# Tail keys of the attention's AV product as half-height matmuls, in a T5-bias attention and FFN kernel

## The chip, the cores and the metric

The kernel runs on one core of one Trainium2 chip. The metric is the device time of one execution in microseconds; the median of several runs is compared. Reported beside it are the span of the profiled execution (first to last instruction) and the clock that TensorE was granted.

## The reference

Eight batches of eight heads, 576 positions and 64 values a head, T5-style bias by distance, then a two-layer FFN with a leaky ReLU. Cut to what is computed:

```python
scores = q @ k.transpose(0, 1, 3, 2) / sqrt(64)          # (8, 8, 576, 576)
scores = scores + bias_table[bucket(abs(i - j))]         # constant beyond a distance of 128
attn = softmax(scores)
x = (attn @ v).transpose(0, 2, 1, 3).reshape(4608, 512)
h = x @ w_in                                             # 512 -> 2048
out = maximum(0.01 * h, h) @ w_out                       # 2048 -> 512, float32
```

## The kernel before

**Tiling of the attention.** Work goes by pairs of heads: `items` lists 32 pairs, `n` from 0 to 31, four to a batch. Scores stand transposed, keys on partitions and queries along the free dimension. The 576 keys are four chunks of 128 (`NJ = 4`) and a tail of 64 (`SL`). Per pair, `score(n, u)` makes six units: units 0 to 3, one for each full chunk, are two matmuls (one for each head) on partitions 0 to 63 and 64 to 127 of `kt` and `qt` (the head dimension is 64); unit 4 is the last 64 queries against the full chunks; unit 5 is the tail keys of both heads, 64 partitions each, against all queries. `expo(n, u)` is the exponential on ScalarE: units 0 to 4 go to the buffer `at`, unit 5 to `at4`, where the lower 64 partitions hold head 0's tail keys and the upper 64 head 1's. The bias is multiplied in afterwards by `band(n, c)` on VectorE. There are two `at`/`at4` buffers, used by turns.

**AV.** `av(n, e)` makes the output of one head `e`: five blocks of 128 queries (`NJ + 1`), each a chain of four matmuls over full key chunks (`L480`) and one over the tail keys (`L482`), 65 columns wide: 64 values and a column of ones that gives the softmax sum. The tail matmul uses all 128 partitions of `at4` and a `v4` whose half for the other head is zero. The chain is closed by the tail (`stop=True`). The output lies in one PSUM bank, `ps_o`, of a pool of one; only in batch 0 does head 1 take a bank `ps_om` of the pool `m` of three. `norm(n, e)` on VectorE takes the reciprocal of the sums (`L491`) and multiplies (`L492`) into `opair`. The result is turned into `xT` by a DMA on SP's queue (`x_dma`) or by TensorE (`x_pe`, `L506`, with a copy `L510`).

**FFN.** Nine tiles `T` of 512 tokens. `ffn_in(T, f)` is four matmuls of 512 columns (`L523`) into a bank of the pool `m`; ScalarE turns it into `gt` (`L528`). `ffn_out(T, ts, i)` is a quarter of the 16 matmuls (`L535`) that make 128 tokens of the output, in another bank of `m`; VectorE copies it out (`L540`) and SP stores it.

**Transposes of q and k.** `rows`, `turn_by_pe` (TensorE, `L395`, through two banks of `m`) or, for pairs 10 and later, `turn_by_dma` (SP), then `take_turned` (`L407`) and `apart` (`L411`).

**Order.** The order of all engines is made by the class `Plan`: every task has an engine, a cost in microseconds, tasks that must precede it, a rank, and PSUM slots that it takes and gives (`S`: the two score slots of two banks each, `O`: the bank `ps_o`, `M`: the banks of pool `m`). `order()` always takes the task that can start first by these numbers, and by rank among equals; so FFN blocks fill the time between a pair's tasks. `plan_pair(n)` adds a pair's scores (from pair 4 on in three tasks of two units), exponentials, bands, the two AVs (cost 0.78 each, after everything of the pair is done) and divisions. `user_before(n)` names the pair whose `at` buffer pair `n` uses again.

Of the kernel before, what the change touches and what calls it, by code (L numbers as in the profile page):

```python
# [10 lines left out]
FP32 = mybir.dt.float32  # L11
# [25 lines left out]
class Plan:  # L37
# [8 lines left out]
    def add(self, engine, cost, after, go, rank, take=(), give=(), tail=0.0, at=None):  # L46
        t = {"engine": engine, "cost": cost, "after": list(after), "go": go, "rank": rank, "n": len(self.tasks),
             "take": list(take), "give": list(give), "tail": tail, "end": at, "start": at}
        if at is None:
            self.tasks.append(t)  # L50
        return t
# [71 lines left out]
def kernel(  # L123
# [10 lines left out]
    nc = tc.nc  # L134

    B, H, S, D = q.shape
# [4 lines left out]
    P = 128  # L141
    n_pairs = H // 2
    NJ = S // P
    SL = S - NJ * P
# [19 lines left out]
    ps_o_pool = ctx.enter_context(tc.tile_pool(name="ps_o", bufs=1, space=bass.MemoryType.PSUM))  # L164
    ps_m_pool = ctx.enter_context(tc.tile_pool(name="ps_m", bufs=3, space=bass.MemoryType.PSUM))
# [11 lines left out]
    NBUF = 2  # L177
# [5 lines left out]
    v4 = [per.tile([P, n_pairs, 2, D + 1], BF16, name=f"v4_{i}") for i in range(NBUF)]  # L183
# [179 lines left out]
    items = [(b, p) for b in range(B) for p in range(n_pairs)]  # L363
    N = len(items)
    NQT = 3
    qts, kts, opairs, prs, turned, scores, outs = {}, {}, {}, {}, {}, {}, {}
# [7 lines left out]
    def x_by_dma(n):  # L374
        return n_pairs + 2 <= n < N - 1 and n != 2 * n_pairs - 1
# [40 lines left out]
    def at_buf(n):  # L416
        if n == 2:
            return spare
        i = n if n < 2 else (n + 1) % 2
        return at_[i], at4_[i]  # L420
# [4 lines left out]
    def score(n, u):  # L425

        qt, kt = qts[n], kts[n]
        ps = scores[n, u] = ps_s_pool.tile([P, 2, 512], FP32, name="ps_s")
        if u < NJ:
            for e in range(2):  # L430
                r = slice(e * D, (e + 1) * D)
                nc.tensor.matmul(ps[:, e, :], lhsT=kt[r, u * P : (u + 1) * P], rhs=qt[r, 0:512],  # L432
                                 start=True, stop=True)
        elif u == NJ:
            for c in range(NJ):
                nc.tensor.matmul(ps[:, 0, c * P : (c + 1) * P], lhsT=kt[:, c * P : (c + 1) * P],  # L436
                                 rhs=qt[:, S : S + P], start=True, stop=True)
        else:
            nc.tensor.matmul(ps[:, 0, :], lhsT=kt[:, S : S + P], rhs=qt[:, 0:512], start=True, stop=True)  # L439
            nc.tensor.matmul(ps[:, 1, 0:SL], lhsT=kt[:, S : S + P], rhs=qt[:, 512:S], start=True, stop=True)  # L440
# [14 lines left out]
    def band(n, c):  # L455
# [8 lines left out]
            m = mirrored(hk[:, 2 * p : 2 * p + 2, :], lo - (c - 1) * P, hi - (c - 1) * P)  # L464
        nc.vector.tensor_tensor(out=o, in0=o, in1=m, op=ALU.mult)  # L465

    def av(n, e):

        b, p = items[n]
        i = b % NBUF  # L470
        at, at4 = at_buf(n)
        if b == 0 and e == 1:
            ps = ps_m_pool.tile([P, NJ + 1, D + 1], FP32, name="ps_om", tag="m")
        else:
            ps = ps_o_pool.tile([P, NJ + 1, D + 1], FP32, name="ps_o", tag="ps_o")
        outs[n, e] = ps
        for ic in range(NJ + 1):
            for c in range(NJ):
                o = (e * NJ + c) * S + ic * P
                nc.tensor.matmul(ps[:, ic, :], lhsT=at[:, o : o + P], rhs=vn[i][:, c, 2 * p + e, :],  # L480
                                 start=(c == 0), stop=False)
            nc.tensor.matmul(ps[:, ic, :], lhsT=at4[:, ic * P : (ic + 1) * P], rhs=v4[i][:, p, e, :],  # L482
                             start=False, stop=True)

    def norm(n, e):

        ps = outs.pop((n, e))
        if e == 0:
            opairs[n] = op_pool.tile([P, NJ + 1, 2 * D], BF16, name="opair")
        rcp = rc_pool.tile([P, NJ + 1, 1], FP32, name="rcp")  # L490
        nc.vector.reciprocal(rcp, ps[:, :, D : D + 1])  # L491
        nc.vector.tensor_tensor(out=opairs[n][:, :, e * D : (e + 1) * D], in0=ps[:, :, 0:D],  # L492
                                in1=rcp.to_broadcast([P, NJ + 1, D]), op=ALU.mult)
# [37 lines left out]
    def ffn_out(T, ts, i):  # L531
        if i == 0:
            ys[T, ts] = ps_m_pool.tile([P, DM], FP32, name="pm2", tag="m")
        for f in range(4 * i, 4 * i + 4):
            nc.tensor.matmul(ys[T, ts], lhsT=gts[T][:, f, ts * P : (ts + 1) * P], rhs=w_out_sb[:, f, :],  # L535
                             start=(f == 0), stop=(f == n_fc - 1))
# [11 lines left out]
    add = plan.add  # L548
    L = {}
    rowt, cut, sct, ext, avt, nmt, xt, vt = {}, {}, {}, {}, {}, {}, {}, {}  # L550
# [72 lines left out]
    def user_before(n):  # L623
        return None if n < 3 else (n - 3 if n < 5 else n - 2)

    order_s = []

    def plan_pair(n):
        b, p = items[n]
        rank = 10 * n  # L630
        soon = rank - (25 if n == n_pairs - 1 else 0)
        cq, ck, aq, ak = cut[n]
        need = {4: [aq, ck], 5: [ak, cq]}
        units = [[u] for u in range(6)] if n < n_pairs else [[0, 1], [2, 3], [4, 5]]
        ac = [0.95, 0.95, 0.95, 0.95, 0.52, 0.56]
        m = user_before(n)
        before = avt[m] if m is not None else []
        es, ss = {}, []
        for us in units:
            ds = [d for u in us for d in need.get(u, [cq, ck])]  # L640
            if n >= PACE and us[0] == 0:
                j = 4 * (n - 4) - LEAD
                if j >= 0:
                    ds.append(("in", j // n_fc, j % n_fc))
            t = add("PE", 0.3 * len(us), ds + before + order_s[-1:],
                    lambda us=us: [score(n, u) for u in us], rank + (-25 if n < n_pairs else 2), take=["S"] * len(us))
            order_s.append(t)
            ss.append(t)
            for u in us:
                es[u] = add("ACT", ac[u], [t], lambda u=u: expo(n, u), rank + 2, give=["S"])  # L650
        sct[n] = ss
        cost = [0.43, 0.56, 0.56, 0.48, 0.25]
        bt = [add("DVE", cost[c], [es[u] for u in ([c], [c], [c], [3, 4], [5])[c]] + [L["hk", 0 if n == 0 else 1]],
                  lambda c=c: band(n, c), soon + 3) for c in range(NJ + 1)]
        done = list(es.values()) + bt + [vt[b]]
        old = xt.get(n - 2, [])
        avs, nms = [], []
        for e in range(2):
            k = "M" if b == 0 and e == 1 else "O"
            avs.append(add("PE", 0.78, done, lambda e=e: av(n, e), soon + 4, take=[k]))  # L660
            nms.append(add("DVE", 0.68, [avs[-1]] + old + nms, lambda e=e: norm(n, e), soon + 3, give=[k]))
        avt[n] = avs
        if x_by_dma(n):
            xt[n] = [add("SP", 0.1, nms, lambda: x_dma(n), soon + 4, tail=6.0)]
            nmt[n] = xt[n]
        else:
            xt[n] = [add("PE", 0.3, nms, lambda: x_pe(n), soon + 4, take=["M"])]
            nmt[n] = [add("DVE", 0.45, xt[n], lambda: x_copy(n), soon + 3, give=["M"])]
# [11 lines left out]
    def plan_ffn(T):  # L680
        last = (T * TT + TT - 1) // S
        need = [t for p in range(n_pairs) for t in nmt[last * n_pairs + p]]
        acts = []
        for f in range(n_fc):
            i = ins[T, f] = add("PE", 0.866, need + [L["w_in", int(f >= n_fc // 2)]] + (oin[T - 2] if T > 1 else []),
                                lambda f=f: ffn_in(T, f), 10000 + T * 64 + f * 4, take=["M"])
            acts.append(add("ACT", 0.54, [i], lambda f=f: ffn_act(T, f), 10000, give=["M"]))
        oin[T] = []
        for ts in range(TT // P):
            last_p = []  # L690
            for i in range(4):
                rank = 10000 + (T + 1) * 64 + (ts * 4 + i) * 4 + 2
                last_p = [add("PE", 0.866, acts + [L["w_out", i // 2]] + last_p, lambda ts=ts, i=i: ffn_out(T, ts, i),
                              rank, take=["M"] if i == 0 else [])]
                oin[T] += last_p
            y = add("DVE", 0.69, last_p + ([yts[-4]] if len(yts) > 3 else []), lambda ts=ts: ffn_y(T, ts), 0, give=["M"])
            yts.append(add("SP", 0.1, [y], lambda ts=ts: ffn_store(T, ts), 10000, tail=2.5))
# [7 lines left out]
    for T in range(n_tt):  # L705
        plan_ffn(T)
# [40 lines left out]
```

## Time and profile before

| | us |
|---|---|
| runs | 393.38, 394.59, 392.37 |
| median of the three | 393.38 |
| profiled execution | 393.96 |
| its span | 392.2 |
| granted TensorE clock over the span | 0.984 |
| full-chunk AV matmuls from the two `at` buffers into `ps_o` (`L480`) | 1180 instructions |
| tail matmuls of the same (`L482`) | 295 instructions |

Times in the profile are microseconds unless marked ns. Engines: PE is TensorE's matmuls, PEld its weight loads (they overlap with PE), DVE is VectorE, ACT is ScalarE, POOL is GpSimd, SP is SyncE, and SPq a DMA queue's issuer. `L480` is line 480 of the kernel before. A line `ps_o<-vn,at 128*128 128x65` names output and inputs, the rows and columns of the array that are used, and the moving operand. Matmuls are pipelined: the length of one is not the distance from one to the next. A `<-` behind an idle time names what ended it.

### The profile page before, as it was taken

The page shows a single profiled execution, that of the slowest core. Times are in us where ns is not written, and L with a number is a line of the kernel's source. Part 1 is how long each engine was busy: PE and PEld are TensorE (multiplying, and loading weights), DVE is VectorE, ACT ScalarE, POOL GpSimd, SP SyncE. Part 2 cuts the span into 40 slices and gives each one's busy share as a digit, 9 for nine tenths or more (in the row PEclk, how much of TensorE's full clock was granted, in tenths as well). Part 3 has the DMA queues.
Part 4 walks back from the last instruction along what each step waited for, and adds up shares of the span by engine and source line. Part 5 has one row for each costly group of instructions (what it writes and reads, how often), then busy time and mean ns, then how long its engine had stood idle before and what let it go on. Part 6 is the DMA issues. An engine that isn't in the chain of part 4 may idle for free.

```text
span 392.2 us, 8305 instructions
## 1 busy us (share of the span) xinstructions
PE 376.5 (96%) x3388; PEld 191.6 (49%) x3388; DVE 202.8 (52%) x539; ACT 243.6 (62%) x345; POOL 68.8 (18%) x112
## 2 busy tenths in 40 slices
PE   7849899999999999999999999999999999999995
PEld 2437355555455454545545555555555444444442
DVE  6637657886776666668567755555433201001021
ACT  3936689548966898688777766666675333333300
POOL 7267404043005201600700220000000000000000
PEclk8978999999999999999999999999999999999998
DMA  7969999779949984997995591111111010101012
GB/s 127 217 112 180 207 207 166 132 104 173 172 98 111 179 117 79 159 158 111 122 157 123 80 133 45 45 43 45 46 43 46 31 51 27 55 27 53 28 53 80
DMA packets 102741, 40.62 MB, mean 104 GB/s; under 512 B 81704, under 2 KB 97072, under 8 KB 102704
## 3 DMA queue, kind: packets, MB, share of 16 engines
q0 software_dynamic: 48512, 17.47, 40.8%
q1 hardware_dynamic: 53984, 22.33, 28.4%
q8 instruction: 26, 0.43, 0.4%
q10 hardware_dynamic: 208, 0.29, 0.3%
q14 instruction: 11, 0.09, 0.1%
HBM read 37.69 MB, written 9.45 MB: 120 GB/s over the span
## 4 chain that ended last, share of the span: by engine, by line
PE 89%; SPq 3%; DVE 2%; DMA 2%; ACT 1%; POOL 1%; issue 0%; DVEq 0%; POOLq 0%
PE pm L535 32%; PE pm L523 32%; PE ps_o L480 10%; PE ps_s L432 8%; PE ps_o L482 2%; SPq L312 2%; PE ps_s L436 2%; PE ps_s L439 2%; DMA tab<-in_bias_table_dram 1%; DMA first<-in_v_dram 1%; ACT at L446 1%; DVE opair L492 1%; POOL vn L333 1%; DVE at L465 1%; PE ps_t L395 0%; PE ps_om L480 0%
## 5 line engine op out<-in xcount | busy, mean ns | idle before, releaser
L523 PE MATMUL pm<-xT,w_in_sb 128*128 128x512 bf16 x576 | 145.0, 379 | 1.5 <-ACT gt L528 1.0
L535 PE MATMUL pm<-w_out_sb,gt 128*128 128x512 bf16 x576 | 143.3, 379 | 0.0
L446 ACT ACTIVATE at<-ps_s 128x1024 bf16<-128x1024 f32 x124 | 120.2, 1023 | 26.8 <-PE ps_s L432 25.6
L528 ACT ACTIVATE gt<-pm 128x512 bf16<-128x512 f32 x144 | 86.1, 601 | 75.4 <-PE pm L523 74.5
L535 PEld LDWEIGHTS <-gt 128*128 128x128 bf16 x576 | 52.7, 98 | 66.0 <-issue 8.9
L523 PEld LDWEIGHTS <-w_in_sb 128*128 128x128 bf16 x576 | 52.5, 98 | 64.2 <-issue 6.9
L465 DVE TENSOR_TENSOR at<-at,hk 128x768 bf16<-128x768 bf16 (+3 forms) x155 | 68.0, 453 | 24.5 <-ACT at L446 14.6
L540 DVE COPY y<-pm 128x512 f32<-128x512 f32 x36 | 24.8, 690 | 82.2 <-PE pm L535 81.7
L480 PEld LDWEIGHTS <-at 128*128 128x128 bf16 x1240 | 53.4, 99 | 22.2 <-issue 8.9
L480 PE MATMUL ps_o<-vn,at 128*128 128x65 bf16 x1180 | 54.7, 195 | 4.5 <-POOL vn L333 4.5
L482 PE MATMUL ps_o<-v,at 128*128 128x65 bf16 x295 | 48.1, 195 | 0.1
L203 POOL DMA_DIRECT2D vn<-in_v_dram x24 | 21.2, 896 | 136.3 <-PE ps_o L482 125.1
L432 PE MATMUL ps_s<-qt,kt 64*128 64x512 bf16 x256 | 40.7, 389 | 0.9 <-ACT at L453 0.3
L491 DVE RECIPROCAL rcp<-ps_o 128x5 f32<-128x5 f32 x60 | 11.7, 194 | 50.2 <-PE ps_o L482 50.0
L482 PEld LDWEIGHTS <-at 128*128 128x128 bf16 x310 | 30.7, 99 | 0.5 <-issue 0.5
L492 DVE TENSOR_TENSOR opair<-ps_o,rcp 128x320 bf16<-128x320 f32 x60 | 29.5, 492 | 2.3 <-DVE rcp L491 0.2
L448 ACT ACTIVATE at<-ps_s 128x512 bf16<-128x512 f32 x31 | 18.5, 598 | 12.1 <-PE ps_s L436 12.0
L407 DVE COPY qt<-tu 128x576 bf16<-128x576 bf16 x22 | 14.6, 666 | 14.8 <-PE ps_s L440 12.9
L453 ACT ACTIVATE at<-ps_s 128x576 bf16<-128x576 f32 x31 | 20.1, 649 | 0.0
L432 PEld LDWEIGHTS <-kt 64*128 64x128 bf16 x256 | 8.2, 94 | 20.8 <-issue 17.8
L407 DVE COPY kt<-tu 128x576 bf16<-128x576 bf16 x22 | 14.3, 652 | 0.0
L436 PEld LDWEIGHTS <-kt 128*128 128x128 bf16 x128 | 9.7, 99 | 6.9 <-ACT at L446 0.5
(77 smaller groups left out, 203.1 us busy)
## 6 DMA issues: line engine op xcount, KB each, us to landing
out_dram<-y SPq DMA_DIRECT2D x36, 256.0 KB, 2.1
qn<-in_q_dram POOLq DMA_DIRECT2D x14, 288.0 KB, 10.2
kn<-in_k_dram POOLq DMA_DIRECT2D x14, 288.0 KB, 11.5
vn<-in_v_dram POOLq DMA_DIRECT2D x28, 128.0 KB, 6.4
w_in_sb<-in_moe_w_in_dram POOLq DMA_DIRECT2D x2, 1024.0 KB, 9.5
w_out_sb<-in_moe_w_out_dram POOLq DMA_DIRECT2D x2, 1024.0 KB, 17.9
first<-in_v_dram SPq DMA_DIRECT2D x4, 256.0 KB, 7.0
hk<-u_row SPq DMA_DIRECT2D x1, 576.0 KB, 7.2
```

What stands on the lines that cost most here:

```text
L203: nc.gpsimd.dma_start(out=vn[i][:, c, :, 0:D], in_=v[b, :, c * P : (c + 1) * P, :].rearrange("h s d -> s h d"),)
L407: copy(out=t[:, 0:S].rearrange("p (r c) -> p r c", c=NC), in_=src)
L432: nc.tensor.matmul(ps[:, e, :], lhsT=kt[r, u * P : (u + 1) * P], rhs=qt[r, 0:512], start=True, stop=True)
L446: nc.scalar.activation(at[:, :, u, 0:512], ps, AF.Exp, scale=scale)
L465: nc.vector.tensor_tensor(out=o, in0=o, in1=m, op=ALU.mult)
L480: nc.tensor.matmul(ps[:, ic, :], lhsT=at[:, o : o + P], rhs=vn[i][:, c, 2 * p + e, :], start=(c == 0), stop=False)
L482: nc.tensor.matmul(ps[:, ic, :], lhsT=at4[:, ic * P : (ic + 1) * P], rhs=v4[i][:, p, e, :], start=False, stop=True)
L492: nc.vector.tensor_tensor(out=opairs[n][:, :, e * D : (e + 1) * D], in0=ps[:, :, 0:D], in1=rcp.to_broadcast([P, NJ + 1, D]), op=ALU.mult)
L523: nc.tensor.matmul(pm[:, j * w : (j + 1) * w], lhsT=w_in_sb[:, c, f * P : (f + 1) * P], rhs=xT[c][:, t0 : t0 + w], start=(c == 0), stop=(c ...
L528: nc.scalar.activation(gts[T][:, f0 : f0 + TT // w, 0:w], pms.pop((T, f0)).rearrange("p (j t) -> p j t", t=w), AF.Prelu, bias=0.0, scale=1 ...
L535: nc.tensor.matmul(ys[T, ts], lhsT=gts[T][:, f, ts * P : (ts + 1) * P], rhs=w_out_sb[:, f, :], start=(f == 0), stop=(f == n_fc - 1))
L540: nc.vector.tensor_copy(out=y, in_=ys[T, ts])
```

## The change

For pairs 4 to 30 (`by_rows(n)`: batch 1 up to the last pair but one) the ten tail matmuls of a pair are taken out of the two AVs and become one block `av_tail(n)`, which runs first. In it the heads go by turns: head 0 uses partitions 0 to 63 of `at4` and `v4` and writes `ps_o`, head 1 uses partitions 64 to 127 and writes `ps_om`, a bank of pool `m`. The first tail matmul of each bank opens it (`start`), the AVs over the full chunks add to it and close it. The block is attached to the planned task of the next pair's second score block (units 2 and 3), which takes the slots `O` and `M` for it and has 0.15 added to its cost; the AVs have to come after it, head 1 ahead of head 0, at cost 0.62. Pairs 0 to 3 and 31 keep the old form. Besides, a task of `ffn_out` no longer waits for all 16 activations of its tile in the plan: quarters 0 to 2 wait for the first 12, quarter 3 for all 16.

```diff
+    def by_rows(n):
+        return n_pairs <= n < N - 1
+
+    def av_open(n, e):
+        if e == 1 and (by_rows(n) or items[n][0] == 0):
+            outs[n, e] = ps_m_pool.tile([P, NJ + 1, D + 1], FP32, name="ps_om", tag="m")
+        else:
+            outs[n, e] = ps_o_pool.tile([P, NJ + 1, D + 1], FP32, name="ps_o", tag="ps_o")
+
+    def av_tail(n):
+        b, p = items[n]
+        at4 = at_buf(n)[1]
+        for e in range(2):
+            av_open(n, e)
+        for ic in range(NJ + 1):
+            for e in range(2):
+                r = slice(e * SL, (e + 1) * SL)
+                nc.tensor.matmul(outs[n, e][:, ic, :], lhsT=at4[r, ic * P : (ic + 1) * P],
+                                 rhs=v4[b % NBUF][r, p, e, :], start=(ic == 0), stop=False)
+
     def av(n, e):
...
+        whole = not by_rows(n)
+        if whole:
+            av_open(n, e)
+        ps = outs[n, e]
         for ic in range(NJ + 1):
             for c in range(NJ):
                 o = (e * NJ + c) * S + ic * P
                 nc.tensor.matmul(ps[:, ic, :], lhsT=at[:, o : o + P], rhs=vn[i][:, c, 2 * p + e, :],
-                                 start=(c == 0), stop=False)
-            nc.tensor.matmul(ps[:, ic, :], lhsT=at4[:, ic * P : (ic + 1) * P], rhs=v4[i][:, p, e, :],
-                             start=False, stop=True)
+                                 start=whole and c == 0, stop=not whole and ic == NJ and c == NJ - 1)
+            if whole:
+                nc.tensor.matmul(ps[:, ic, :], lhsT=at4[:, ic * P : (ic + 1) * P], rhs=v4[i][:, p, e, :],
+                                 start=False, stop=True)
...
-            t = add("PE", 0.3 * len(us), ds + before + order_s[-1:],
-                    lambda us=us: [score(n, u) for u in us], rank + (-25 if n < n_pairs else 2), take=["S"] * len(us))
+            tail = by_rows(n - 1) and us[0] == 2
+            t = add("PE", 0.3 * len(us) + (0.15 if tail else 0.0), ds + before + order_s[-1:] + (tail_of[n - 1] if tail else []),
+                    lambda us=us, tail=tail: [[score(n, u) for u in us], av_tail(n - 1) if tail else None],
+                    rank + (-25 if n < n_pairs else 2), take=["S"] * len(us) + (["O", "M"] if tail else []))
+            if tail:
+                for a in avt[n - 1]:
+                    a["after"].append(t)
...
+        tail_of[n] = [es[NJ + 1], bt[NJ], vt[b]]
...
-        for e in range(2):
-            k = "M" if b == 0 and e == 1 else "O"
-            avs.append(add("PE", 0.78, done, lambda e=e: av(n, e), soon + 4, take=[k]))
+        for e in (1, 0) if by_rows(n) else (0, 1):
+            k = "M" if (b == 0 or by_rows(n)) and e == 1 else "O"
+            avs.append(add("PE", 0.62 if by_rows(n) else 0.78, done, lambda e=e: av(n, e), soon + 4,
+                           take=[] if by_rows(n) else [k]))
...
-                last_p = [add("PE", 0.866, acts + [L["w_out", i // 2]] + last_p, lambda ts=ts, i=i: ffn_out(T, ts, i),
+                last_p = [add("PE", 0.866, acts[: max(4 * i + 4, 12)] + [L["w_out", i // 2]] + last_p, lambda ts=ts, i=i: ffn_out(T, ts, i),
```

More of the change, by code (lines that the diff above doesn't have):

```diff
@@ L471, in av @@
         at, at4 = at_buf(n)
[L472 to L476, printed above, removed]
+        whole = not by_rows(n)
+        if whole:
+            av_open(n, e)
+        ps = outs[n, e]
         for ic in range(NJ + 1):
@@ L480, in av @@
                 nc.tensor.matmul(ps[:, ic, :], lhsT=at[:, o : o + P], rhs=vn[i][:, c, 2 * p + e, :],
-                                 start=(c == 0), stop=False)
-            nc.tensor.matmul(ps[:, ic, :], lhsT=at4[:, ic * P : (ic + 1) * P], rhs=v4[i][:, p, e, :],
-                             start=False, stop=True)
+                                 start=whole and c == 0, stop=not whole and ic == NJ and c == NJ - 1)
+            if whole:
+                nc.tensor.matmul(ps[:, ic, :], lhsT=at4[:, ic * P : (ic + 1) * P], rhs=v4[i][:, p, e, :],
+                                 start=False, stop=True)
     def norm(n, e):
         ps = outs.pop((n, e))
-        if e == 0:
+        if n not in opairs:
             opairs[n] = op_pool.tile([P, NJ + 1, 2 * D], BF16, name="opair")
@@ L624, in user_before @@
         return None if n < 3 else (n - 3 if n < 5 else n - 2)
-    order_s = []
+    order_s, tail_of = [], {}
     def plan_pair(n):
```

## The prediction

> **What bounds the kernel now.** I read the page's busy table and slices first, then TensorE's busy time by stretches, then its waits.
>
> ```profile
> span 392.2 us, 8305 instructions
> PE 376.5 (96%) x3388; PEld 191.6 (49%) x3388; DVE 202.8 (52%) x539; ACT 243.6 (62%) x345; POOL 68.8 (18%) x112
> PE   7849899999999999999999999999999999999995
> PEclk8978999999999999999999999999999999999998
> PE 89%; SPq 3%; DVE 2%; DMA 2%; ACT 1%; POOL 1%; issue 0%; DVEq 0%; POOLq 0%
> ```
>
> ```profile
> 30.00:60.00 30.00, 27.50 (x361) 16.82 (x359) 19.80 (x55) 21.94 (x31) 13.32 (x19) 0.97 1.40 198
> 58.00:300.00 242.00, 241.87 (x2430) 124.58 (x2430) 156.04 (x415) 180.44 (x252) 39.72 (x53) 1.00 0.83 110
> 300.00:385.00 85.00, 85.00 (x442) 39.53 (x441) 11.20 (x19) 25.08 (x42) 0.00 (x0) 1.00 0.11 41
> ```
>
> The columns after the length of a stretch are the busy times of PE, PEld, DVE, ACT and POOL, then the granted clock. From 58 us on TensorE is never without a matmul, at full clock, until the last stores; TensorE makes 89% of the chain that ended last. ACT has a quarter of the middle stretch free, DVE a third. So a TensorE microsecond taken away after 58 us is a microsecond of the end, provided that the other engines keep up with the new order. The waits of TensorE from 58 us on are one row, and that one stands at its very beginning:
>
> ```profile
> PE pm L523 <- DVE qt L407: 0.5, 1, 0.5
> ```
>
> **What an AV block costs today.** The page's mean of 195 ns for a 65-column matmul is a latency, since matmuls are pipelined; the price is the distance between starts. The timeline of one pair shows it (start, length, line, operation, count):
>
> ```profile
> 150.67 0.60 PE L432 MATMUL ps_s<-qt,kt 64*128 64x512 bf16 x4
> 151.20 1.04 PE L523 MATMUL pm<-xT,w_in_sb 128*128 128x512 bf16 x4
> 152.08 0.28 PE L480 MATMUL ps_o<-vn,at 128*128 128x65 bf16 x4
> 152.20 0.19 PE L482 MATMUL ps_o<-v,at 128*128 128x65 bf16 x1
> 152.23 0.28 PE L480 MATMUL ps_o<-vn,at 128*128 128x65 bf16 x4
> ...
> 152.83 1.03 PE L535 MATMUL pm<-w_out_sb,gt 128*128 128x512 bf16 x4
> 153.79 0.61 PE L432 MATMUL ps_s<-qt,kt 64*128 64x512 bf16 x4
> 154.33 0.30 PE L480 MATMUL ps_o<-vn,at 128*128 128x65 bf16 x4
> ```
>
> One head's AV is 25 matmuls from 152.08 to 152.83: 0.75 us, 0.030 each, its weight load hidden. The tail matmul (L482) costs the same 0.03 as a full one, though half of its 128 rows multiply zeros. A pair has ten: 0.30 us.
>
> **What the change removes and adds on TensorE.** In 27 pairs (4 to 30) those ten become ten 64-row matmuls, two heads by turns, upper and lower half of the array, into two banks. The count of instructions is unchanged, so the gain hangs on one thing: do two 64-row matmuls on different halves run at once? The scores already do it:
>
> ```profile
> 150.67 0.39 PE L432 MATMUL ps_s<-qt,kt 64*128 64x512 bf16 x2
> 150.66 0.11 PEld L432 LDWEIGHTS <-kt 64*128 64x128 bf16 x4 [0.42 <-issue]
> L432 PE MATMUL ps_s<-qt,kt x12: 376/382/388, 150.7 to 159.4; 64*128 64x512 bf16 x12
> L432 PEld LDWEIGHTS <-kt 64*128 64x128 bf16 x256 | 8.2, 94 | 20.8 <-issue 17.8 <-DVE kt L407 0.7 <-ACT kt L407 0.4
> ```
>
> Two score matmuls of at most 0.388 us each (min/median/max in the row) fit into 0.39 together, so they start within hundredths of each other; four loads of 94 ns fit into 0.11, so starts of loads are no bound either. Five such twos of 65 columns at 0.030 make 0.15 us instead of 0.30. Bounds: 0.15 below (each half must still stream five times 65 columns at the 0.030 of the rows; no row is shorter for 65 columns) and 0.30 above (ten starts one after another, as today). I take 0.15, because the score rows are the only ones with 64-row matmuls. Then a pair's AV goes from 2 x 0.75 = 1.50 to 0.15 + 40 x 0.030 = 1.35, and 27 x 0.15 = **4.05 us** leave a TensorE that is the bound.
>
> Does the new block cost a change of array shape? Four score matmuls take 151.20 - 150.67 = 0.53, where two streams of 512 columns take half of the 152.08 - 151.20 = 0.88 of four full ones, 0.44: leaving the 64-row form costs 0.09. Likewise the four matmuls from 152.83 take 0.96 before a score block, 0.08 more than 0.88. The Trainium skill, "TensorEngine Tiling (Array Packing)", Key Properties, says that changing the tiling mode drains the array; these rows agree, with 0.09 a change, and by that rule tail matmuls among full ones would lose more than they gain. The new block stands directly behind a 64-row score block, so the exit is only postponed: no change of form is added. I price this at nothing; if the tail paid one all the same, 27 x 0.09 = 2.4 us.
>
> **What moves.** From the order of the changed kernel's instructions I read, for a middle pair: score block (units 0 and 1), three FFN blocks, score block (2 and 3), tail of the previous pair, its AV of head 1 and head 0, two FFN blocks, units 4 and 5, two FFN blocks. Before, it was score block, FFN, AV, FFN, score block, AV, two FFN, units 4 and 5, two FFN. A pair now has mostly seven FFN blocks instead of six, so attention ends later and less FFN is left; the sum of the work is the same, as long as no wait appears. The queued waits:
>
> *ScalarE.* Units 2 and 3 need the banks that the exponentials of units 0 and 1 give back.
>
> ```profile
> 98.31 0.60 ACT L528 ACTIVATE gt<-pm 128x512 bf16<-128x512 f32 x1
> 99.17 0.60 ACT L528 ACTIVATE gt<-pm 128x512 bf16<-128x512 f32 x1 [0.27 <-PE pm L523]
> 99.66 1.94 ACT L446 ACTIVATE at<-ps_s 128x1024 bf16<-128x1024 f32 x2
> 101.47 0.62 ACT L528 ACTIVATE gt<-pm 128x512 bf16<-128x512 f32 x1
> 105.92 0.59 ACT L448 ACTIVATE at<-ps_s 128x512 bf16<-128x512 f32 x1
> 106.40 0.66 ACT L453 ACTIVATE at<-ps_s 128x576 bf16<-128x576 f32 x1
> 106.93 1.29 ACT L528 ACTIVATE gt<-pm 128x512 bf16<-128x512 f32 x2
> ```
>
> Two exponentials hold ScalarE for 101.47 - 99.66 = 1.81, an FFN activation for 99.66 - 99.17 = 0.49, the two short exponentials for 0.48 and 0.53. Between the score blocks TensorE has 3 x 0.88 = 2.64 against 1.81 + 0.49 = 2.30 (before: 153.79 - 151.20 = 2.59). A pair with seven input blocks asks 2 x 1.81 + 1.01 + 7 x 0.49 = 8.06 of ScalarE in some 9.1 of TensorE (seven blocks 6.16, two score blocks 1.06, units 4 and 5 about 0.5, AV 1.35). It fits, with 0.3 to spare at the tightest place.
>
> *Banks.* Head 1's sums now take one of the FFN's three banks from the tail until its division: 0.15 + 20 x 0.03, and 0.65 for reciprocal and product (54.58 - 53.94 below). Behind the waiting tail would stand both AVs and the FFN. In the densest pairs three activations are ahead of it: the first is done 1.81 + 0.49 = 2.30 after the first score block, the tail comes at 2.64 + 0.44 = 3.08. In exchange the two heads no longer share one bank, so no AV follows a division closely.
>
> *VectorE, early.* In pairs 4 to 9 transposed queries and keys pass through the same three banks, and VectorE empties them.
>
> ```profile
> 53.94 0.20 DVE L491 RECIPROCAL rcp<-ps_o 128x5 f32<-128x5 f32 x1 [1.80 <-PE ps_o L482]
> 54.17 0.49 DVE L492 TENSOR_TENSOR opair<-ps_o,rcp 128x320 bf16<-128x320 f32 x1
> 54.58 0.35 DVE L385 COPY pr<-qn 96x768 bf16<-96x768 bf16 x1
> 57.32 0.75 DVE L407 COPY qt<-ps_t 128x576 bf16<-128x576 bf16 x1
> 57.99 0.45 DVE L510 COPY xT<-ps_tx 128x576 bf16<-128x576 bf16 x1
> 58.13 1.89 PE L523 MATMUL pm<-xT,w_in_sb 128*128 128x512 bf16 x8 [0.51 <-DVE qt L407]
> 58.35 0.55 DVE L465 TENSOR_TENSOR at<-at,hk 128x768 bf16<-128x768 bf16 x1
> 58.82 0.75 DVE L407 COPY kt<-ps_t 128x576 bf16<-128x576 bf16 x1
> ```
>
> The worst place of the new order is behind pair 4's AV: two transposes, an FFN block, units 4 and 5, the transposes of pair 4's result, two transposes of pair 7. VectorE does from the AV's end 0.2 + 0.65 (division) + 0.47 (band) + 2 x 0.67 (copies) = 2.66; TensorE arrives at the second of those last transposes about 0.3 us early, and at a later FFN block about as early again: 0.6 us of stall, where before had the 0.51 of the row. I add 0.1 (bounds -0.5, the old stall gone, to +1.5, each of three such places losing its 0.5). SP's queue holds the same transposes and stores in another order, pairs being further apart; POOL's order is the same. The relaxed condition of the FFN's second half moves only the planned order: nothing.
>
> **The sum.** The profiled execution took 393.96 us (span 392.2 and 1.76 around it). 393.96 - 4.05 + 0.1 + 0.2 (my allowance for two waits of the size of the tightest margin not quite kept) = 390.2. The three runs shown have the median 393.38, 0.58 less: **389.6 us** on that footing, 1.0% less.
>
> **Rivals.**
> *The tail does not overlap* (0.12). If ten starts stand in a row at 0.030 as today's 65-column matmuls do, the tail costs 0.30, nothing is gained, and the result is 393.4 + 0.3 = 393.7. No row has two short 64-row matmuls; against it stand the 0.39 and 0.11 above. The Trainium skill, "TensorE: Matmul & The Clock Gate", Part 1, gives a floor of about 25 ns from start to start however small the matmul; were that to hold across the halves, the tail would take 0.25 and the result would be about 392.3, an estimate from that page. The two scores within 0.39 speak against it.
> *One more drain a pair* (0.05): 389.6 + 2.4 = 392.0.
> *Slower: the FFN's bank* (0.11). With head 1 holding one bank and a half-done output sum another, input blocks have one left and run at the pace of block, activation, block: 0.88 + 0.49 + two exponentials queued ahead. If the activation waits behind the 1.81, TensorE loses up to 1.81 + 0.49 - 0.88 = 1.4 at one place of a pair. From 0.15 a pair on it eats the gain; 0.4 a pair gives 389.6 + 27 x 0.4 = 400, 0.25 a pair 396.4. For it: ScalarE is the tightest margin above. Against: in the order the first block behind the AVs finds head 1's division done 0.2 us later and the third bank free.
> *More than forecast* (0.04): the early stall gone too, below 388.6.
>
> **Chances.** The forecast, gain within some 0.9 us, has 0.68. About 0.5% (2 us) is what a measurement of this kernel can tell. Faster by more, below 391.4: forecast and better case: 0.72. Within 0.5%: no overlap, the drain, and the stalls up to 0.2 a pair: 0.18. Slower: 0.10, the rest of the bank rival. The range runs from 388.5 to 392.3: the early stall gone and no allowance needed at one end (389.6 - 0.6 - 0.2, and the last 0.3 for the spread of the median); at the other a half-overlapping tail (27 x 0.075 = 2.0) with half of the early bound (0.7), which takes in the drain too. It leaves out most of no overlap and the bank rival.
>
> **What would show it.** Right: in the timeline of after, ten tail matmuls between the score block and head 1's AV, with head 1's first full matmul some 0.15 + 0.09 us behind the end of the scores' stream; TensorE busy through every stretch after 60 us; 27 x 0.15 less matmul time from 60 us on. Wrong: head 1's AV 0.3 us or more behind the tail's first start (no overlap); a wait of the tail or of an FFN block for ScalarE that is repeated through the pairs (bank); idle time of more than 1.5 us between 53 and 75 us (VectorE). If the middle shows full busy time and the total still does not fall, the price of the tail is wrong.

## The result

| kernel | median of its runs, us | profiled execution, us | span |
|---|---|---|---|
| before | 393.44 | 393.96 | 392.2 |
| after | 389.17 | 389.1 | 387.3 |

The ratio is 0.9887, with a 95% interval from 0.9868 to 0.9907: 1.1% or some 4.3 us less. The forecast was 389.6 us.

The page of after, its busy table, slices and granted clock:

```profile
span 387.3 us, 8302 instructions
PE 372.1 (96%) x3388; PEld 188.8 (49%) x3388; DVE 202.9 (52%) x539; ACT 241.7 (62%) x345; POOL 68.6 (18%) x112
PE   6859899999999999999999999999999999999995
PEclk9968999999999999999999999999999999999999
PE 88%; DVE 3%; SPq 3%; DMA 2%; ACT 1%; POOL 1%; issue 0%; DVEq 0%; POOLq 0%
```

TensorE has 4.4 us less to do and is as full as before; it still makes the chain that ended last. The stretches of after say the same (columns as before: PE, PEld, DVE, ACT, POOL, clock):

```profile
58.00:300.00 242.00, 241.84 (x2418) 123.37 (x2414) 154.51 (x408) 176.61 (x250) 39.94 (x53) 1.00 0.86 109
300.00:380.00 80.00, 80.00 (x467) 38.04 (x460) 12.85 (x25) 25.53 (x42) 0.00 (x0) 1.00 0.12 42
```

In the list of waits no wait of TensorE is left from 58 us on (holes too short for that list are counted further down). The timeline of one pair of after shows the block itself:

```profile
156.69 0.61 PE L432 MATMUL ps_s<-qt,kt 64*128 64x512 bf16 x4
157.13 0.19 PE L485 MATMUL ps_o<-v,at 64*128 64x65 bf16 x1
157.13 0.19 PE L485 MATMUL ps_om<-v,at 64*128 64x65 bf16 x1
157.16 0.19 PE L485 MATMUL ps_o<-v,at 64*128 64x65 bf16 x1
157.16 0.19 PE L485 MATMUL ps_om<-v,at 64*128 64x65 bf16 x1
...
157.25 0.19 PE L485 MATMUL ps_om<-v,at 64*128 64x65 bf16 x1
157.38 0.79 PE L500 MATMUL ps_om<-vn,at 128*128 128x65 bf16 x20
158.01 0.77 PE L500 MATMUL ps_o<-vn,at 128*128 128x65 bf16 x20
158.61 1.89 PE L556 MATMUL pm<-w_out_sb,gt 128*128 128x512 bf16 x8
```

Read the starts, not the lengths: a matmul of each head starts at the same time, the next two start 0.03 later, and the five twos fill 0.15. The score block ends 0.44 after its start (0.53 before) because it no longer pays for leaving the 64-row form; the first full matmul stands 0.69 behind the score block's start, where it stood 154.33 - 153.79 = 0.54 before. So the tail costs a pair 0.15 us net.

Where the 4.86 us between the two profiled executions lie: the two orders are the same up to an FFN block that waits for ScalarE, which starts at 45.82 before and at 45.17 after. These 0.65 us are the beginning's own spread, no work of the change. Behind that point the spans differ by (392.2 - 45.82) - (387.3 - 45.17) = 4.25 us (4.18 with unrounded spans), which is about what the medians differ by.

### The profile page after: what moved, and what is told of

Read it like the earlier page. It is cut to its first block, busy times and chain, and to the rows that moved or that the text cites. A ratio compares the mean times of both kernels' runs of the same rounds, so it can differ in the third digit from the quotient of the medians.

```text
span 387.3 us, 8302 instructions
## 1 busy us (share of the span) xinstructions
PE 372.1 (96%) x3388; PEld 188.8 (49%) x3388; DVE 202.9 (52%) x539; ACT 241.7 (62%) x345; POOL 68.6 (18%) x112
## 4 chain that ended last, share of the span: by engine, by line
PE 88%; DVE 3%; SPq 3%; DMA 2%; ACT 1%; POOL 1%; issue 0%; DVEq 0%; POOLq 0%
PE pm L544 32%; PE pm L556 32%; PE ps_s L432 8%; PE ps_om L500 5%; PE ps_o L500 5%; PE ps_s L436 2%; PE ps_s L439 2%; SPq L312 1%; DMA tab<-in_bias_table_dram 1%; DVE opair L513 1%; DMA first<-in_v_dram 1%; PE ps_o L485 1%; ACT at L446 1%; DVE at L465 1%; POOL vn L333 1%; PE ps_t L395 0%
## 5 line engine op out<-in xcount | busy, mean ns | idle before, releaser
L544 PE MATMUL pm<-xT,w_in_sb 128*128 128x512 bf16 x576 | 140.6, 380 | 1.1 <-ACT gt L549 1.0
L556 PE MATMUL pm<-w_out_sb,gt 128*128 128x512 bf16 x576 | 138.8, 380 | 0.0
L549 ACT ACTIVATE gt<-pm 128x512 bf16<-128x512 f32 x144 | 84.4, 606 | 62.1 <-PE pm L544 61.1
L500 PEld LDWEIGHTS <-at 128*128 128x128 bf16 x1240 | 42.8, 99 | 6.8 <-issue 4.9
L500 PE MATMUL ps_o<-vn,at 128*128 128x65 bf16 x640 | 27.0, 196 | 4.1 <-POOL vn L333 4.1
L512 DVE RECIPROCAL rcp<-ps_om 128x5 f32<-128x5 f32 x31 | 6.0, 195 | 38.6 <-PE ps_om L500 37.6
L500 PE MATMUL ps_om<-vn,at 128*128 128x65 bf16 x600 | 24.6, 196 | 0.0
L513 DVE TENSOR_TENSOR opair<-ps_o,rcp 128x320 bf16<-128x320 f32 x33 | 16.2, 492 | 1.1
L513 DVE TENSOR_TENSOR opair<-ps_om,rcp 128x320 bf16<-128x320 f32 x31 | 15.2, 492 | 1.3 <-DVE rcp L512 0.3
L439 PE MATMUL ps_s<-qt,kt 128*128 128x512 bf16 x32 | 12.4, 387 | 0.9 <-ACT at L446 0.9
```

What stands on the lines that cost most here:

```text
L544: nc.tensor.matmul(pm[:, j * w : (j + 1) * w], lhsT=w_in_sb[:, c, f * P : (f + 1) * P], rhs=xT[c][:, t0 : t0 + w], start=(c == 0), stop=(c ...
L549: nc.scalar.activation(gts[T][:, f0 : f0 + TT // w, 0:w], pms.pop((T, f0)).rearrange("p (j t) -> p j t", t=w), AF.Prelu, bias=0.0, scale=1 ...
```

## The experiments

Two theories were to be told apart: that the gain is the overlap of the two 64-row halves, or that it is the new order with its second bank and the relaxed FFN condition.

**Full height again.**

```diff
-                r = slice(e * SL, (e + 1) * SL)
+                r = slice(0, P)
```

> The changed kernel with one edit: the tail matmuls use all 128 partitions of at4 and v4 (whose other half is zero) again, two banks, heads by turns, same place; the order on every engine is that of the changed kernel. Theory (the gain is that two 64-row matmuls run at once): the tail block needs ten starts at 0.030 instead of 5 x 0.030, 0.30 against 0.15, so 27 x 0.15 = 3.9 us come back: 389.2 + 3.9 = 393.1 us (392.6 to 393.6). Rival (the new order, the second bank for head 1 and the vanished stall of the early part make the gain): stays at 389.2, at most 390.

Measured: 393.81 us, ratio to before 1.001 (0.9999 to 1.0021), 0.2 above the range expected. Its timeline:

```profile
111.13 0.60 PE L432 MATMUL ps_s<-qt,kt 64*128 64x512 bf16 x4
111.67 0.20 PE L485 MATMUL ps_o<-v,at 128*128 128x65 bf16 x1
111.71 0.20 PE L485 MATMUL ps_om<-v,at 128*128 128x65 bf16 x1
111.75 0.19 PE L485 MATMUL ps_o<-v,at 128*128 128x65 bf16 x1
...
111.96 0.20 PE L485 MATMUL ps_om<-v,at 128*128 128x65 bf16 x1
112.00 0.38 PE L500 MATMUL ps_om<-vn,at 128*128 128x65 bf16 x7
```

The starts stand 0.03 to 0.04 apart, the block takes 0.33, and the first AV matmul comes 0.87 behind the score block's start instead of 0.69. 27 x 0.18 = 4.9 on top of after's 389.17 would be 394.0; measured is 393.81. With every other part of the change in place nothing of the gain is left. The rival of the order and the banks falls; the overlap is the gain.

**Head by head.**

```diff
-        for ic in range(NJ + 1):
-            for e in range(2):
+        for e in range(2):
+            for ic in range(NJ + 1):
```

> The changed kernel with the tail's two loops exchanged: five matmuls of head 0 in the lower half, then five of head 1 in the upper half; all else the same. If matmuls start in program order (theory), only one of them, where the heads meet, has a partner: nine starts at 0.030 = 0.27 instead of 0.15, 27 x 0.12 = 3.2 us: 392.4 us (391.8 to 393.0). Rival (the two halves of the array run apart, each from its own part of the queue): stays at 389.2.

Measured: 389.98 us, ratio to before 0.9921 (0.9903 to 0.9939). The expectation of the theory (392.4) missed; the rival was near. The timeline:

```profile
110.67 0.60 PE L432 MATMUL ps_s<-qt,kt 64*128 64x512 bf16 x4
111.12 0.22 PE L485 MATMUL ps_o<-v,at 64*128 64x65 bf16 x2
111.15 0.20 PE L485 MATMUL ps_om<-v,at 64*128 64x65 bf16 x1
111.18 0.19 PE L485 MATMUL ps_o<-v,at 64*128 64x65 bf16 x1
111.19 0.19 PE L485 MATMUL ps_om<-v,at 64*128 64x65 bf16 x1
...
111.26 0.22 PE L485 MATMUL ps_om<-v,at 64*128 64x65 bf16 x2
111.41 0.33 PE L500 MATMUL ps_om<-vn,at 128*128 128x65 bf16 x5
```

In the program all five matmuls of `ps_o` stand ahead of all five of `ps_om`. In the trace the first of `ps_om` starts at 111.15, ahead of the third of `ps_o`. TensorE started matmuls of one half ahead of earlier ones of the other. The block is only 0.05 longer (0.74 to the first AV matmul against 0.69): 27 x 0.05 = 1.35, which would give 390.5; measured is 389.98. The Trainium skill, "TensorE: Matmul & The Clock Gate", Part 3, has matmuls start and end strictly in program order; for matmuls on different halves of the array this trace disagrees. So taking turns in the program is worth about 1 us (0.8 by the medians, with intervals that overlap those of after, and 1.35 by the starts); being on different halves is worth the rest.

**Among full matmuls.** The tail goes between head 1's AV, which then opens its own bank, and head 0's. The `start` and `stop` flags that go with it are left out here.

```diff
-        if whole:
+        if whole or e == 1:
             av_open(n, e)
...
+        if e == 1 and not whole:
+            av_tail(n)
...
-                    lambda us=us, tail=tail: [[score(n, u) for u in us], av_tail(n - 1) if tail else None],
+                    lambda us=us, tail=tail: [[score(n, u) for u in us], None],
```

> The changed kernel with the same ten 64-row matmuls put between the AVs of head 1 and head 0, that is among 128-row matmuls, instead of directly behind the 64-row score block (head 1's first full matmul opens its bank, the tail opens head 0's). Planned order otherwise the same. Theory (each change of array form costs some 0.09): one way in and one way out more for each of 27 pairs, 27 x 0.19 = 5.1 us: 394.3 us (393.5 to 395). Rival (the drain is hidden or the halves need no change of form for 65 columns): 389.2 to 389.8. Between them, about 391.7, if only one direction costs.

Measured: 395.32 us, ratio to before 1.0055 (1.0039 to 1.0072), 6.15 us above after and 0.3 above the range expected. The timeline:

```profile
111.79 0.60 PE L432 MATMUL ps_s<-qt,kt 64*128 64x512 bf16 x4
112.33 0.79 PE L499 MATMUL ps_om<-vn,at 128*128 128x65 bf16 x20
113.05 0.20 PE L484 MATMUL ps_o<-v,at 64*128 64x65 bf16 x1
113.05 0.20 PE L484 MATMUL ps_om<-v,at 64*128 64x65 bf16 x1
...
113.18 0.19 PE L484 MATMUL ps_om<-v,at 64*128 64x65 bf16 x1
113.31 0.47 PE L499 MATMUL ps_o<-vn,at 128*128 128x65 bf16 x10
```

The heads overlap as before (0.26 from the block's start to head 0's AV, its way out included), but head 0's AV now starts 113.31 - 111.79 = 1.52 behind the score block and not 158.01 - 156.69 = 1.32. 27 x 0.20 = 5.4 of the 6.15; the profiled execution of this kernel took 394.5, which is 5.4 above after's. Two changes of form, about 0.20 together, cost more than the 0.15 that the overlap brings: the place behind a 64-row block makes the difference between 1.1% less and 0.6% more than before.

**The relaxed FFN condition, undone in after and alone in before.** Only the argument that changes is shown of the line.

```diff
-acts[: max(4 * i + 4, 12)] + [L["w_out", i // 2]]
+acts + [L["w_out", i // 2]]
```

> The changed kernel with the one other edit undone: in the plan every quarter of the FFN's second half waits for all 16 activations again. The order moves: pair 11 then has one FFN block instead of three between its two score blocks, 0.96 us of TensorE against 1.81 + about 0.3 that ScalarE needs for the exponentials. Theory: one stall of 1.2 us there, 390.4 us (389.7 to 391.0), nothing at the other pairs. Rival (the relaxed condition carries part of the gain through the whole kernel): 391.5 or more. If nothing waits for it: 389.2.

Measured: 390.50 us, ratio to before 0.9932 (0.9911 to 0.9954), 1.3 us above after by the medians; the intervals of the two ratios do not quite touch. From its list of waits and its timeline at pair 11:

```profile
PE ps_s L432 <- ACT at L446: 0.5, 1, 0.5
```

```profile
107.84 0.61 PE L432 MATMUL ps_s<-qt,kt 64*128 64x512 bf16 x4
108.38 1.04 PE L544 MATMUL pm<-xT,w_in_sb 128*128 128x512 bf16 x4
109.51 0.39 PE L432 MATMUL ps_s<-qt,kt 64*128 64x512 bf16 x2
110.43 0.39 PE L432 MATMUL ps_s<-qt,kt 64*128 64x512 bf16 x2 [0.52 <-ACT at L446]
```

The block and wait stand where they were expected. Unit 3 starts 110.43 - 109.51 = 0.92 behind unit 2, which takes 0.22 elsewhere; with the late start of unit 2 that is about 0.9 of the 1.3. The rest is not attributed.

With the same condition relaxed in the kernel before, and nothing else:

```diff
-acts + [L["w_out", i // 2]]
+acts[: max(4 * i + 4, 12)] + [L["w_out", i // 2]]
```

> The kernel before with only the relaxed condition of the FFN's second half (quarters 0 to 2 planned after 12 activations); no tail block, no second bank. Theory (this edit moves only the order of a TensorE that is busy anyway): 393.4 us, at best the early stall of 0.5 us less: 392.8 to 393.7. Rival (it makes part of the gain): 392 or less.

Measured: 393.70 us against 393.65 of before in the same session, ratio 1.0001 (0.9989 to 1.0013). The early stall stayed:

```profile
PE pm L523 <- DVE qt L407: 0.5, 1, 0.5
```

So this edit brings nothing by itself; in after 1.3 us of the gain depend on it, and about 0.9 of them are the one hole at pair 11.

**Behind the first score block.**

```diff
-            tail = by_rows(n - 1) and us[0] == 2
+            tail = by_rows(n - 1) and us[0] == 0
```

> The changed kernel with the tail behind the next pair's first score block instead of the second; the AVs follow directly. The changes of array form are as many as in the changed kernel. In the planned order most pairs then have nine FFN blocks, and the FFN work that is ready runs out: pair 12 has none at all, 2.7 us of TensorE against 3.62 + 1.01 = 4.6 of ScalarE's exponentials, pairs 16, 20, 24 and 28 have five or six. Theory: the price of the tail is the same, one stall of 2 to 2.5 us at pair 12: 391.5 us (390.8 to 392.5). Rival (any place behind a 64-row block is as good): 389.2.

Measured: 397.69 us, ratio to before 1.0092 (1.0065 to 1.0119): far above the 391.5 (390.8 to 392.5) expected. The stall at pair 12 was there, with something behind it. Stretches of this kernel, the last two rows cut where the granted clock changes:

```profile
120.00:126.00 6.00, 6.00 (x56) 3.05 (x55) 3.34 (x8) 1.92 (x4) 0.00 (x0) 1.00 0.38 92
126.00:132.00 6.00, 3.79 (x55) 2.12 (x51) 4.83 (x13) 5.91 (x8) 4.87 (x6) 0.85 1.26 126
132.00:138.00 6.00, 5.78 (x56) 3.38 (x54) 2.19 (x7) 1.25 (x3) 2.76 (x5) 0.58 2.10 119
138.00:144.00 6.00, 6.00 (x34) 2.88 (x33) 2.60 (x7) 5.72 (x11) 0.00 (x0) 1.00 1.31 195
126.85:130.24 3.39, 1.97 (x15) 0.84 (x13) 2.61 (x7) 3.30 (x5) 3.11 (x4) 1.00 0.83 102
130.24:137.06 6.82, 5.81 (x58) 3.73 (x59) 3.95 (x12) 2.56 (x4) 4.52 (x7) 0.50 2.39 131
```

TensorE idled 2.2 us between 126 and 132, as worked out. But the first 3.39 - 1.97 = 1.4 us of it came within 3.4 us, and behind them, from 130.24 to 137.06, the granted clock was 0.50. The AV of one head took 1.09 there, where after has 0.63:

```profile
132.03 1.28 PE L500 MATMUL ps_om<-vn,at 128*128 128x65 bf16 x20
133.12 1.29 PE L500 MATMUL ps_o<-vn,at 128*128 128x65 bf16 x20
134.22 1.90 PE L544 MATMUL pm<-xT,w_in_sb 128*128 128x512 bf16 x4
```

Half the clock over 5.81 us of matmul time would be some 2.9 us more at most, an estimate. In five of the six runs of this kernel the granted clock over the span was 0.978 to 0.983 and the time 397.06 to 398.10; in the sixth the clock was 0.99 and the time 394.41. That run has no trace; its numbers agree with about 3 us for the fall of the clock, which then did not come in every run. The list of waits has two further entries of more than 1 us that after does not have:

```profile
PE pm L544 <- DMA xT<-opair: 1.8, 3, 0.9
PE ps_o L485 <- DVE at L465: 1.3, 3, 0.6
```

Of the second, 0.6 lies at pair 12. Counted by starts, which include what the list misses of each hole, pair 12 takes 5.7 us more than the same work elsewhere, the three waits for `xT` take 2.3 and the two other waits for VectorE 1.1; after's early holes of 0.7 (below) are not there. That is 8.4 of the 8.5 us above after. The price of the tail block itself is the same here (0.25 from its first start to head 1's AV in the median pair, as in after); this order lacks FFN work at pair 12 and waits for results that are still being transposed at others.

## Why the prediction held, point by point

**TensorE as the bound.** Right: 241.84 of 242.00 us busy in after too.

**The tail at 0.15 and not 0.30.** Right: 0.15 in the timeline, net of the way out. This step carries the result: the run with full-height tails gives the time of before. Summing starts over the traces behind 45 us, an old tail took 0.0301, so 270 of them 8.12 us; the new blocks took, net of the way out, 27 x 0.154 = 4.15. That is 3.97 us gained, where the prediction had 4.05 from rounded starts.

**No change of form added.** Right, and it decides the sign: among full matmuls the price was 0.20 a pair. The rival of one more drain had been put at 0.09 a pair; where a block stands alone it is two.

**ScalarE and the banks.** Right: no wait. The margin at the tightest place, worked out as 0.3, was enough in every pair of after; with one FFN block instead of three between the score blocks (strict condition) the wait for ScalarE appeared at once.

**The early part.** The mechanism was there; the balance was small and on the other side. Behind pair 4's AV the transposes of its result started at 59.71, 0.28 behind the end of unit 5. The next twelve transposes took 0.74 instead of 0.52, of which 0.10 is the way into the 64-row form and 0.13 a hole behind the sixth of them:

```profile
59.40 0.19 PE L440 MATMUL ps_s<-qt,kt 128*128 128x64 bf16 x1
59.71 0.44 PE L527 MATMUL ps_tx<-ident,opair 128*128 128x128 bf16 x5
59.98 0.80 PE L395 MATMUL ps_t<-ident,pr 96*128 96x96 bf16 x12
60.72 0.60 PE L432 MATMUL ps_s<-qt,kt 64*128 64x512 bf16 x4
```

With a hole of 0.11 in the FFN block behind (at 61.92) that is 0.52 of the 0.6 expected; a further 0.21 came at 88.53, where an FFN block waited for the copy of `xT`: 0.73 in all. But before lost more there than its one row of 0.51 said. The five transposes ahead of that stall, in before's timeline:

```profile
57.16 0.45 PE L506 MATMUL ps_tx<-ident,opair 128*128 128x128 bf16 x5
58.13 1.89 PE L523 MATMUL pm<-xT,w_in_sb 128*128 128x512 bf16 x8 [0.51 <-DVE qt L407]
```

They held TensorE for 0.97, against 59.98 - 59.71 = 0.27 for the five in after. The 0.70 more is a hole, of which the row shows 0.51: the list of waits counts idle time behind the modelled ends of matmuls and so misses the first 0.2 of it. With another hole of 0.12 ahead of the transposes at 67.20 before lost 0.82, and the balance is 0.73 - 0.82 = -0.1 where +0.1 was expected. The terms that were mis-sized are this one (0.2) and the unused allowance (0.2); the tails' gain was 0.1 smaller than forecast, and 0.1 of the 4.18, on the other side, is not attributed. Together this is the 0.4 by which 389.6 was too high.

**The rivals.** That the tail does not overlap fell by the timeline, one drain more by the tail's place, the bank rival by the list of waits. The floor of 25 ns from start to start that the Trainium skill gives ("TensorE: Matmul & The Clock Gate", Part 1) does not hold across the halves: the rows at 157.13 start together.

## What to carry to other kernels

In this kernel a 65-column matmul on half of the rows stood 0.03 us from the next on the same half, as full ones do; with a partner on the other half, in another bank, the two took 0.03 together when they took turns in the program, and little more when they stood five matmuls apart (0.17 for the ten). Two halves that write the same bank were not tried. Put such a block next to work that has the same array form already: alone among full matmuls it lost 0.20 us a visit, more than the 0.15 that it won. And where TensorE is the bound, price a matmul by the distance of starts in the timeline, and look for holes in the starts too, since a wait of up to 0.2 us does not show as idle time.

## What the runs showed of the hardware

- Matmuls on different halves of the array do not keep program order: `ps_om`'s first started ahead of `ps_o`'s third though it stands behind `ps_o`'s fifth, and from the first start to the last (111.29, the second of the row at 111.26) the ten took 0.17 instead of 9 x 0.03 = 0.27.
- In the profiled run with the tail behind the first score block, 1.4 us of idle time within 3.4 us (the longest wait row 0.71) came ahead of a fall of the granted clock to 0.50, which lasted 6.8 us. By an estimate from the 5.81 us of matmul time in it, this cost up to 2.9 us, against 2.2 us of idle time at that pair.
